# The second expert gets a token list of its own; the table's weight columns are written ahead of the last weight matrix

## The chip, the cores and the metric

The kernel runs on one core of a Trainium2 chip. TensorE (PE) multiplies, VectorE (DVE) and ScalarE (ACT) work elementwise, GpSimd (POOL) works elementwise and issues the gathers and scatters, SyncE (SP) only issues transfers. The metric is the device time of one launch in microseconds (us).

## The reference

The input is q, k, v of 4 batches, 8 heads, 768 steps, 64 per head. Three layers follow one another; the third is the one that the change touches.

```python
# 1: attention with a decaying state; x is its output, 3072 tokens x 512
state = gamma * state + k[t] (outer) v[t];  y[t] = scale * q[t] @ state
# 2: soft mixture, 8 experts x 4 slots
logits = x @ phi;  d = softmax(logits, over tokens)
slot_out[e] = relu((d.T @ x)[e] @ w1[e]) @ w2[e]
x = softmax(logits, over slots) @ slot_out              # rank 32: c @ slot_out
# 3: two of 8 experts for each token
noisy = x @ w_gate + log1p(exp(x @ w_noise)) * noise
top2, weights = the two largest of noisy, softmax of the two
for e in range(8):
    for k in range(2):
        mask = top2[:, k] == e
        out[mask] += weights[mask, k] * (relu(x[mask] @ w1[e]) @ w2[e])
```

## The kernel before, in words

Layers 1 and 2 fill the first 170 us and are not changed. Since x is `c @ slot_out`, the kernel never forms x for layer 3: a table in DRAM (`ctab`) holds for each token its 32 slot weights c and, in 8 more columns, its weight for each expert. G[e] = slot_out @ w1[e] (`g_dot`, with `V1[e]` as the loaded w1[e]) has 32 rows; an expert's hidden layer is the gathered rows of c times G[e].

**Routing** (lines 664 to 741). Matmuls give the noisy logits; DVE finds both experts of each token (`sels`, `tops`); a matmul with constant matrices (`pp`, line 723) numbers the tokens of each expert. ACT, POOL and DVE make the two weights, and SP writes the 8 weight columns (`wsl`) into the table with two transfers (line 741). SP has issued the loads of V1[0], V1[1], V2[0] and V1[2] (2 MB each, V2 in four pieces; lines 647 to 650) ahead of that write; `V2[e]` is w2[e]. V1[0] and V1[1] lie in the ring of buffers `ringa`, V1[2] in `ringp`, which has two.

**Lists** (`lists`, line 819, and `lists_all`, line 845). An expert's list holds its tokens in blocks of 128. It is made by comparing the place of each token with a table (`oh`, three DVE instructions), by marking the block (`bm`, `bt`), and by 24 small matmuls into `pli`; `ls` are the token numbers. Expert 0 has a list of its own (line 1066). The other seven are made at once by `lists_all`, in two passes of 24 matmuls, on DVE and POOL; an entry says too whether the token's other expert comes earlier (`base`, from `order`, `by_turn`, `lead`, `late`), since an expert either writes an output row or adds to it. `order` sorts experts 3 to 7 by their counts.

**Blocks.** Expert 0 has six blocks of 128 and one of 64 in three groups (g = 0, 1, 2). `fetch(e, g)` gathers the table's rows by indirect transfers on POOL's queue, one for each block (line 923). `turn(e, g)` casts and splits them into two parts (ACT, then `st` on DVE), transposes them on PE (`ptc`) and copies them back (ACT, `cts`). `hidden(e, g)` multiplies by G[e] (`phc`), and ACT (relu) and DVE (`hhl`, the remainder) take each result out. `main(e, g)` is, for each block, 8 steps (kf) of three matmuls of 512 columns: `hhl` by the high part `wh` of V2 (lines 1030, 1032) and by its low part `wl` (line 1031). `split_hi` (ACT) and `split_lo` (DVE) make `wh` and `wl` from V2 in four pieces. Then ACT scales by the weight (`yo`), and POOL scatters the rows to the output (line 1005).

**Order.** A planner arranges each engine's instructions by its own costs; `after(ins)` makes what stands in the block follow `ins` where both run on one engine, without a wait. Each engine then runs in that order. `HOOK[e, b, kf]` calls a function when the matmuls of expert e, block b, step kf are written down. Before the change `lists_all` starts ahead of expert 0's blocks (line 1096) and goes on at (0,1,4) and (0,2,2); the second of these also calls the fetches of expert 1. `turn(0, 2)` hangs at (0,0,4). `fill` writes matmuls on a constant whose result nobody reads: F4 = 16 of them after `g_dot(0)` (line 687), FA = 6 and FT = 3 around `g_dot(2)` (lines 1079 to 1082). `gs0`, the spread form of G[0], is made from `gw` (lines 1069 to 1074) after expert 0's list; for the other experts 16 small transfers on SP do it (`gs<-gr`, line 765).

Of the kernel before, what the change touches and what calls it, by code (L numbers as in the profile page):

```python
# [21 lines left out]
P = 128  # L22
# [5 lines left out]
E = 8  # L28
# [13 lines left out]
F1, F2, F3, F4 = 2, 0, 0, 16  # L42
FA, FT = 6, 3
# [4 lines left out]
TZ = 0, 4  # L48
# [59 lines left out]
def kernel(ctx: ExitStack, tc: tile.TileContext, q, k, v, phi, w1, w2,  # L108
# [458 lines left out]
    with rctx, bctx:  # L567
# [88 lines left out]
        first = parts.tile([P, 2, NCH], F16, name="first")  # L656
# [27 lines left out]
        nc.scalar.copy(gr[:, 0], gd)  # L684
        nc.gpsimd.tensor_tensor(gr[:, 1], gd, gr[:, 0], op=OP.subtract)
        with after(mm):
            fill(psB, "pw", F4, 1)
        lo = small.tile([P, NCH, E], F32, name="lo")
# [21 lines left out]
        nc.gpsimd.tensor_tensor(dif, sels[0], sels[1], op=OP.subtract)  # L710
# [13 lines left out]
        ppe = pp[:, :NCH * E].rearrange("p (c e) -> p e c", e=E)[:, 0]  # L724
# [7 lines left out]
        nc.scalar.activation(w[:, 0], w[:, 0], AF.Exp)  # L732
# [6 lines left out]
        nc.gpsimd.tensor_tensor(wsl, wsl, wse, op=OP.add)  # L739
        for r in range(2):  # L740
            nc.sync.dma_start(row_view(r)[:, :, NS:], wsl[64 * r:64 * r + 64])
# [12 lines left out]
    def g_split(pg):  # L754
        gr = cc.tile([P, 2, QF], F32R, name="gr1", bufs=1)
# [11 lines left out]
    def g_one(e):  # L767
        pg = psC.tile([P, QF], F32, name="pg", tag="phc", bufs=4)
        mm = g_dot(e, pg)
        yield mm  # L770
        g_copy(e, g_split(pg))
        yield mm
# [6 lines left out]
    SRC = {}  # L779

    def order():
# [18 lines left out]
        by_turn = cc.tile([P, NCH, E], F16, name="by_turn", bufs=1)  # L800
        nc.gpsimd.tensor_tensor(by_turn, dif, turns[:, None, :].to_broadcast([P, NCH, E]), op=OP.mult)
        lead = cc.tile([P, NCH], F32, name="lead", bufs=1)
        nc.vector.reduce_sum(lead, by_turn, axis=AX.X)
        for i, side in enumerate((OP.is_gt, OP.is_lt)):
            late = cc.tile([P, NCH], F32, name="late")
            nc.gpsimd.tensor_scalar(late, lead, 0.0, float(LATER), op0=side, op1=OP.mult)
            nc.gpsimd.tensor_tensor(base[i], late, col16("base"), op=OP.add)
# [11 lines left out]
    def lists(e, pool, ps, nb, src=None, ahead=()):  # L819
        rv, bv = src or (rr.rearrange("p (e c) -> p e c", e=E)[:, e],  # L820
                         blk.rearrange("p (c e) -> p c e", e=E)[:, :, e])
        bm = pool.tile([P, NCH, nb], F16, name="bm", bufs=1)
# [3 lines left out]
        nc.vector.tensor_tensor(bt[:, :, 0, :], bm, col16("base")[:, :, None].to_broadcast([P, NCH, nb]), op=OP.mult)  # L826
        scaled = nc.scalar.activation(bt[:, :, 1, :], bm, AF.Copy, scale=tokens)
        oh = pool.tile([P, NCH // 8, P, 8], F16, name="oh", bufs=1)
        for c in range(NCH // 8):
            nc.vector.tensor_tensor(oh[:, c], tab, rv[:, None, 8 * c:8 * c + 8].to_broadcast([P, P, 8]),  # L830
                                    op=OP.is_equal)
        hold = [next(a) for a in ahead]
        pl = ps.tile([P, 2, nb], F32, name="pli", tag="pt")
        for c in range(NCH):
            with after(*hold):
                mm = nc.tensor.matmul(pl.rearrange("p a b -> p (a b)"), oh[:, c // 8, :, c % 8],
                                      bt[:, c].rearrange("p a b -> p (a b)"), start=(c == 0), stop=(c == NCH - 1))
        lt = pool.tile([P, nb], F32, name="lt", bufs=1)
        nc.vector.tensor_scalar_add(lt, pl[:, 0, :], float(N))
        ls = pool.tile([P, nb], I32, name="ls", bufs=1)  # L840
        last = nc.vector.tensor_tensor(ls, lt, pl[:, 1, :], op=OP.add)
        LS[e] = FIRST[e] = ls
        return mm, last, scaled

    def lists_all():
        rv = rr.rearrange("p (e c) -> p c e", e=E)
        bv = blk.rearrange("p (c e) -> p c e", e=E)
        pl = psC.tile([P, 2, E, LB], F32, name="pli", tag="pt")
        bm = cc.tile([P, NCH, E, LB], F16, name="bma", bufs=1)
        nc.vector.tensor_tensor(bm, bv[:, :, :, None].to_broadcast([P, NCH, E, LB]),  # L850
                                col16("iotab")[:, None, None, :LB].to_broadcast([P, NCH, E, LB]), op=OP.is_equal)
        for i in range(2):
            rk = cc.tile([P, NCH, E], F16, name="rk")
            nc.vector.tensor_tensor(rk, sels[i], rv, op=OP.mult)
            rs = cc.tile([P, NCH], F32, name="rs")
            nc.vector.reduce_sum(rs, rk, axis=AX.X)
            rh = cc.tile([P, NCH], F16, name="rh")
            nc.vector.tensor_copy(rh, rs)
# [4 lines left out]
            bt = cc.tile([P, NCH, 2, E, LB], F16, name="bta", bufs=1)  # L863
            sb = cc.tile([P, 2, NCH, E], F16, name="sb")
            for a, part in enumerate((base[i], col16("tok"))):
                nc.gpsimd.tensor_tensor(sb[:, a], sels[i], part[:, :, None].to_broadcast([P, NCH, E]),
                                        op=OP.mult)
                eng = nc.gpsimd if a else nc.vector
                eng.tensor_tensor(bt[:, :, a], bm, sb[:, a, :, :, None].to_broadcast([P, NCH, E, LB]), op=OP.mult)
# [5 lines left out]
        lt = cc.tile([P, E, LB], F32, name="lta", bufs=1)  # L875
        nc.vector.tensor_scalar_add(lt, pl[:, 0], float(N))
        ls = cc.tile([P, E, LB], I32, name="lsa", bufs=1)
        nc.vector.tensor_tensor(ls[:, :ES], lt[:, :ES], pl[:, 1, :ES], op=OP.add)
# [33 lines left out]
    def listed(gen):  # L912
        next(gen)
        for g in range(G):
            fetch(1, g)
# [292 lines left out]
```

## Time and profile before

| | |
|---|---|
| runs | 548.7, 548.73, 551.08 us; median 548.73 |
| profiled execution | 550.95 us; span of its instructions 549.1 us |
| PE busy | 511.1 us (93%), mean granted clock 0.961 |
| DVE, ACT, POOL busy | 249.4, 227.6, 247.7 us (45%, 41%, 45%) |
| HBM | 87.89 MB read, 23.43 MB written |

All times below are of the profiled execution, counted from its first instruction. The granted clock is a share of TensorE's full rate. In a timeline row the bracket is the idle time of the engine before the instruction, and what ended it.

### The profile page before, as it was taken

How to read it: one execution, taken by the hardware profiler on the slowest of the kernel's cores; microseconds unless marked ns; L12 is line 12 of the kernel's file. 1: busy time of each engine (PE TensorE's matmuls, PEld its weight loads, DVE VectorE, ACT ScalarE, POOL GpSimd, SP SyncE). 2: the span in 40 equal slices, each digit the busy share in tenths (PEclk: the TensorE clock that was granted, in tenths of full speed). 3: DMA queues.
4: the chain of work that ended last, by engine and by line, in shares of the span. 5: the costliest groups of instructions: out<-in, count | busy, mean ns of one | idle time of the engine just before them, and what ended most of it. 6: DMA issues, size and time to landing. Idle time of an engine off the chain costs nothing.

```text
span 549.1 us, 11659 instructions
## 1 busy us (share of the span) xinstructions
PE 511.1 (93%) x4633; PEld 395.0 (72%) x4633; DVE 249.4 (45%) x505; ACT 227.6 (41%) x496; POOL 247.7 (45%) x245
## 2 busy tenths in 40 slices
PE   5999999998999877969999999999999999999991
PEld 3888788885534456748787788788787877878880
DVE  2878797954032857814415334333324234154100
ACT  3675656542022542325336346345436255164210
POOL 2744644411011357371556667656538544253231
PEclk8899999999997888889999999999999999999996
DMA  9999999998999813153346356456467563563332
GB/s 247 291 305 312 268 308 324 365 407 286 398 408 386 266 43 103 62 191 99 87 153 196 85 177 186 110 157 193 113 167 223 100 178 53 115 155 45 46 44 35
DMA packets 79905, 105.51 MB, mean 192 GB/s; under 512 B 13420, under 2 KB 54892, under 8 KB 79330
## 3 DMA queue, kind: packets, MB, share of 16 engines
q1 hardware_dynamic: 67312, 90.13, 50.8%
q0 software_dynamic: 11856, 14.36, 13.7%
q8 instruction: 38, 0.62, 0.5%
q10 hardware_dynamic: 674, 0.20, 0.3%
q14 instruction: 25, 0.20, 0.1%
HBM read 87.89 MB, written 23.43 MB: 203 GB/s over the span
## 4 chain that ended last, share of the span: by engine, by line
PE 60%; issue 15%; POOL 8%; DMA 7%; DVE 4%; SPq 2%; ACT 2%; POOLq 0%; DVEq 0%; ACTq 0%
PE pyc L1030 9%; PE pyc L1031 9%; PE pyc L1032 9%; POOL out_dram L1005 6%; PE pa L298 4%; PE py L328 4%; PE phc L985 3%; PE ph L559 3%; DMA w<-in_moe_w_dram 3%; PE pS L343 2%; PE pt L286 2%; PE pt L351 2%; PE pt L274 2%; PE py L319 2%; PE po L626 1%
## 5 line engine op out<-in xcount | busy, mean ns | idle before, releaser
L1030 PE MATMUL pyc<-wh,hhl 128*128 128x512 f32 x384 | 153.2, 399 | 1.1 <-ACT yo L1039 1.1
L1031 PE MATMUL pyc<-wl,hhl 128*128 128x512 f32 x384 | 150.9, 393 | 0.0
L1032 PE MATMUL pyc<-wh,hhl 128*128 128x512 f32 x384 | 150.6, 393 | 0.0
L990 DVE SCALAR_TENSOR_TENSOR hhl<-phc,hhl 128x512 fp32r<-128x512 f32 (+1 forms) x112 | 63.3, 606 | 58.2 <-ACT hhl L988 57.8
L1005 POOL DMA_INDIRECT out_dram<-yo,of_second x45 | 70.3, 1562 | 36.0 <-ACT yo L1039 19.9
L1030 PEld LDWEIGHTS pyc<-wh,hhl 128*128 128x128 f32 x384 | 73.1, 190 | 16.0 <-ACT yo L1039 1.9
L1032 PEld LDWEIGHTS pyc<-wh,hhl 128*128 128x128 f32 x384 | 72.7, 189 | 15.1
L1031 PEld LDWEIGHTS pyc<-wl,hhl 128*128 128x128 f32 x384 | 72.9, 190 | 13.7
L966 DVE TENSOR_TENSOR wl<-w,wh 128x1024 fp32r<-128x1024 f32 x32 | 38.9, 1224 | 87.0 <-ACT wh L960 86.1
L1005 POOL DMA_INDIRECT out_dram<-yo,lsa x39 | 41.3, 1060 | 77.8 <-ACT yo L1039 56.3
L988 ACT ACTIVATE hhl<-phc 128x512 fp32r<-128x512 f32 (+1 forms) x112 | 54.6, 549 | 13.3 <-PE phc L985 12.9
L923 POOL DMA_INDIRECT cg<-ctab,of_token x45 | 43.5, 967 | 20.6 <-issue 17.4
L960 ACT CAST wh<-w 128x1024 fp32r<-128x1024 f32 x32 | 33.5, 1052 | 44.5 <-DMA w<-in_moe_w_dram 37.3
L1039 ACT ACTIVATE yo<-pyc,wt 128x512 f32<-128x512 f32 x30 | 20.6, 688 | 69.9 <-PE pyc L1032 66.1
L302 DVE TENSOR_TENSOR am<-pa,cta 128x512 f32<-128x512 f32 x48 | 33.0, 691 | 17.0 <-PE py L328 8.4
L261 POOL TENSOR_TENSOR comp<-raws,cta 64x512 f32<-64x512 f32 x24 | 24.9, 1039 | 30.7 <-PE py L328 14.7
L985 PE MATMUL phc<-cts,gs 128*128 128x256 f32 (+1 forms) x192 | 34.5, 305 | 4.0 <-ACT cts L954 4.0
L261 POOL TENSOR_TENSOR vl<-raws,cta 64x512 f32<-64x512 f32 x24 | 24.9, 1039 | 28.1 <-PE py L328 20.5
L279 DVE TENSOR_TENSOR qT<-pt,cta 64x512 f32<-64x512 f32 x48 | 33.0, 688 | 8.4 <-DMA cta<-in_const_a_dram 6.0
L985 PEld LDWEIGHTS phc<-cts,gs 128*128 128x128 f32 x192 | 29.7, 200 | 9.6 <-ACT cts L954 4.6
L1039 ACT ACTIVATE yo<-pyc,cg 128x512 f32<-128x512 f32 x18 | 12.4, 689 | 43.1 <-PE pyc L1032 39.2
L298 PE MATMUL pa<-qT,kT 64*64 64x128 f32 x768 | 27.4, 282 | 1.1 <-ACT kT L288 1.1
(228 smaller groups left out, 643.8 us busy)
## 6 DMA issues: line engine op xcount, KB each, us to landing
w<-in_moe_w_dram SPq DMA_DIRECT2D x81, 512.0 KB
w<-in_moe_w_dram SPq DMA_DIRECT2D x6, 2048.0 KB
comp<-in_q_dram SPq DMA_DIRECT2D x12, 512.0 KB
raws<-in_k_dram SPq DMA_DIRECT2D x12, 512.0 KB
raws<-in_v_dram SPq DMA_DIRECT2D x12, 512.0 KB
w2q<-in_moe_w_dram SPq DMA_DIRECT2D x8, 512.0 KB
gs<-gr SPq DMA_DIRECT2D x112, 32.0 KB
raws<-in_moe_w_dram SPq DMA_DIRECT2D x2, 1024.0 KB
```

Of the source, the lines that this page charges most:

```text
L261: pool_ins[0] = nc.gpsimd.tensor_tensor(VL[j][rs], RAW[u][1][gs, :, r, :], gv[gs, r, t, :, None].to_broadcast([64, H, D]), op=OP.mult)
L298: mm = nc.tensor.matmul(pa[a][cs, kb, :], KT[j][r, kb, cs], QT[t][r, kb, g, :], start=True, stop=True, skip_group_check=True)
L923: nc.gpsimd.indirect_dma_start(out=cg[:rows(b), i, :], out_offset=None, in_=ctab, in_offset=index(e, b, rows(b)))
L960: ins = nc.scalar.copy(wh, V2[e][:, 1024 * i:1024 * i + 1024])
L966: nc.vector.tensor_tensor(wl, V2[e][:, 1024 * i:1024 * i + 1024], WH[e][i], op=OP.subtract)
L985: nc.tensor.matmul(ph[:, w * i:w * i + w], GS[e][:, kf + i], CT[e, g][:, :w], start=True, stop=True)
L988: relu.append(nc.scalar.activation(h[:, :, :w], pv, AF.Relu))
L990: last = nc.vector.scalar_tensor_tensor(h[:, :, w + t0:w + t0 + 2 * P], pv[:, :, :2 * P], 0.0, h[:, :, :2 * P], op0=OP.max, op1=OP.subtract)
L1005: ins = nc.gpsimd.indirect_dma_start(out=out, out_offset=index(e, b, n, of), in_=y, in_offset=None, bounds_check=N - 1, oob_is_err=False, ...
L1030: nc.tensor.matmul(py, hhl[:, kf, ts], wh, start=(kf == 0), stop=False)
L1031: nc.tensor.matmul(py, hhl[:, kf, ts], wl, start=False, stop=False)
L1032: nc.tensor.matmul(py, hhl[:, kf, tl], wh, start=False, stop=(kf == KF - 1))
```

## The change

The whole of it concerns the stretch from the end of layer 2 to the first blocks of expert 1.

- V2[0] is loaded after the two writes of the weight columns; V1[0] goes to `ringa`, V1[1] and V1[2] to `ringp`.
- `gw` and `gs0` of expert 0 come right after `g_dot(0)` and five fills, ahead of the routing's numbering and of the copies of the counts (`pos`, `cnt`). F4 is 5 instead of 16, five fills (F6) follow `pp`, FA and FT are gone. The ACT instruction of the weights follows the split of G[0].
- POOL makes the weights first; `dif` and two small instructions for `second` (the base of expert 1's list) come after them.
- Expert 1 gets a list by `lists`, with `second` as its base; `apart` takes its two parts. `lists_all` makes the other six (`EJ`), wholly on DVE and ACT (no POOL), in seven steps (`LISTING`), each behind the latest `hidden` on its engine.
- `turn(0, 0)` follows the third cast and the second remainder of V2[0]; the other pieces follow later. The fetches of expert 1 hang at (0,1,3), (0,2,2), (0,3,6), those of expert 2 at (1,2,1); `turn(0, 2)` at (0,1,2).

```diff
-F1, F2, F3, F4 = 2, 0, 0, 16
-FA, FT = 6, 3
+F1, F2, F3, F4, F5, F6 = 2, 0, 0, 5, 0, 5
+LISTING = (0, 1, 6), (0, 2, 3), (0, 2, 5), (0, 4, 3), (0, 4, 6), (0, 5, 3), (1, 0, 4)
-TZ = 0, 4
+TZ = 1, 2
-        for e in range(2):
-            load_w(V1, v1, e, nc.sync, ringa)
-        load_w(V2, v2, 0, nc.sync, ringb)
-        load_w(V1, v1, 2, nc.sync, ringp)
+        for e, ring in enumerate((ringa, ringp, ringp)):
+            load_w(V1, v1, e, nc.sync, ring)
...
             fill(psB, "pw", F4, 1)
+            for g in range(4):
+                gw = psB.tile([P, QF], F32, name="gw", tag="pt")
...
+                nc.scalar.copy(gs0[:, g], gw)
...
-        nc.scalar.activation(w[:, 0], w[:, 0], AF.Exp)
+        with after(split):
+            nc.scalar.activation(w[:, 0], w[:, 0], AF.Exp)
...
         for r in range(2):
-            nc.sync.dma_start(row_view(r)[:, :, NS:], wsl[64 * r:64 * r + 64])
+            written = nc.sync.dma_start(row_view(r)[:, :, NS:], wsl[64 * r:64 * r + 64])
+        with after(written):
+            load_w(V2, v2, 0, nc.sync, ringb)
+        with after(weighed):
+            nc.gpsimd.tensor_tensor(dif, sels[0], sels[1], op=OP.subtract)
+            nc.gpsimd.tensor_scalar(second, selh.rearrange("p (c e) -> p e c", e=E)[:, 0], float(LATER), 0.0,
+                                    op0=OP.mult, op1=OP.add)
+            nc.gpsimd.tensor_tensor(second, second, col16("base"), op=OP.add)
...
+        turns = TURNS[0]
+        nc.vector.tensor_tensor(by_turn, dif, turns[:, None, :].to_broadcast([P, NCH, E]), op=OP.mult)
+        nc.vector.reduce_sum(lead, by_turn, axis=AX.X)
+        for i, side in enumerate((OP.is_gt, OP.is_lt)):
+            nc.vector.tensor_scalar(late, lead, 0.0, float(LATER), op0=side, op1=OP.mult)
+            nc.vector.tensor_tensor(base[i], late, col16("base"), op=OP.add)
+        wide = [P, NCH, EJ, LB]
         for i in range(2):
+            nc.vector.scalar_tensor_tensor(of, sels[1 - i][:, :, 2:], BIG, bv[:, :, 2:], op0=OP.mult, op1=OP.add)
+            nc.vector.tensor_tensor(bm, of[:, :, :, None].to_broadcast(wide), ..., op=OP.is_equal)
+            nc.scalar.activation(bt[:, :, 1], bm, AF.Copy, scale=tokens)
+            yield
+            nc.vector.tensor_tensor(bt[:, :, 0], bm, base[i][:, :, None, None].to_broadcast(wide), op=OP.mult)
             nc.vector.tensor_tensor(rk, sels[i], rv, op=OP.mult)
+                nc.vector.reduce_sum(rh, rk, axis=AX.X)
+            yield
             for c in range(NCH // 8):
                 nc.vector.tensor_tensor(oh[:, c], tab, ..., op=OP.is_equal)
-                nc.gpsimd.tensor_tensor(sb[:, a], sels[i], part[:, :, None].to_broadcast([P, NCH, E]), op=OP.mult)
-                eng = nc.gpsimd if a else nc.vector
-                eng.tensor_tensor(bt[:, :, a], bm, sb[:, a, :, :, None].to_broadcast([P, NCH, E, LB]), op=OP.mult)
             yield
...
+    g1, l0 = g_one(1), lists(0, cc, psC, LB, (first[:, 1, 0], first[:, 0, 0]))
+    next(l0)
+    made = next(l0)
+    with after(*made):
         fetch(0, 0)
+        mm, _ = g1
+        g2 = g_one(2, "pyc", None)
         with after(mm):
+            mm = next(g2)
+        cast = [split_hi(0, i) for i in range(3)]
+        rest = [split_lo(0, i) for i in range(2)]
+        with after(mm):
+            ga = turn(0, 0, [cast[2], rest[1]])
+        with after(*ga):
+            split_lo(0, 2)
...
+        with after(relu[1]):
+            split_hi(0, 3)
+        with after(h0, relu[-1]):
+            split_lo(0, 3)
+            next(g2)
...
         with after(h0, *ga):
+            l1 = lists(1, cc, psC, LB, (first[:, 1, 1], first[:, 0, 1]), second)
+            next(l1)
...
+            HOOK[0, 1, 1] = lambda: [next(l1), apart(1)],
+            HOOK[0, 1, 5] = behind, order, places
+            for at_b in LISTING:
+                HOOK[at_b] = behind, lambda: next(gen)
+            for g, (at_b, kf) in enumerate(((1, 3), (2, 2), (3, 6))):
+                HOOK[0, at_b, kf] = fetch, 1, g
+            HOOK[1, 2, 1] = lambda: [fetch(2, g) for g in range(G)],
```

## Rows read from the trace of the kernel before

**Rows 1.** Windows: busy time by engine, granted clock, DMA share, GB/s.
```profile
core 0: us, PE busy (x) PEld busy (x) DVE busy (x) ACT busy (x) POOL busy (x), PEclk, DMA share, GB/s
199.10:249.70 50.60, 41.79 (x199) 33.73 (x199) 31.94 (x79) 18.19 (x46) 27.42 (x28) 0.84 0.30 100
...
400.00:500.00 100.00, 98.91 (x518) 80.15 (x517) 35.87 (x68) 45.16 (x100) 48.51 (x38) 1.00 0.56 136
```
**Rows 2.** Chain of waits, 160 to 200 us: start, us, what.
```profile
183.78 5.39 DMA ctab<-wsl
...
189.20 2.36 DVE wl L966 x2
...
193.95 2.45 DMA cg<-ctab,ls
...
199.13 0.79 PE pyc L1030
```
**Rows 3.** Windows around the write of the weight columns.
```profile
183.00:189.00 6.00, 4.64 (x65) 3.29 (x66) 4.88 (x11) 4.05 (x8) 1.24 (x3) 0.94 0.99 287
189.00:192.00 3.00, 3.00 (x9) 1.11 (x9) 3.00 (x4) 2.07 (x6) 0.00 (x0) 0.55 0.19 45
```
**Rows 4.** Timeline of POOL: routing's end, first fetches of experts 0 and 1.
```profile
181.39 0.73 POOL L685 TENSOR_TENSOR gr<-gd,gr 128x256 fp32r<-128x256 f32 x1
182.08 0.54 POOL L710 TENSOR_TENSOR dif<-sel,sel 128x192 f16<-128x192 f16 x1
...
192.25 1.40 POOL L923 DMA_INDIRECT cg<-ctab,ls  x1 [7.93 <-DVE wl L966]
193.95 0.99 POOL L923 DMA_INDIRECT cg<-ctab,ls  x1 [0.30 <-issue]
...
232.56 0.99 POOL L923 DMA_INDIRECT cg<-ctab,of_token  x1 [0.30 <-DVE of_second L889]
```
**Rows 5.** Timeline of PE from the list of expert 0 on.
```profile
183.82 1.93 PE L187 MATMUL pg<-w,sotT 128*32 128x256 f32 x32 [0.96 <-ACT cnt L728]
185.69 1.63 PE L836 MATMUL pli<-bt,oh 128*128 128x14 f16 x24
```
**Rows 6.** The same timeline, waits of over 0.7 us after 199.12.
```profile
216.49 0.74 PE L951 MATMUL ptc<-identr,st 128*128 128x128 f32 x3 [3.04 <-DVE st L937]
...
225.38 0.76 PE L872 MATMUL pli<-bta,oh 128*128 128x112 f16 x9 [0.78 <-DVE bta L869]
...
238.72 0.52 PE L951 MATMUL ptc<-identr,st 128*128 128x128 f32 x3 [1.42 <-DVE st L937]
...
243.69 1.43 PE L985 MATMUL phc<-cts,gs 128*128 128x320 f32 x4 [3.56 <-ACT cts L954]
```
**Rows 7.** Windows of three stretches of expert 0's stage.
```profile
198.50:201.90 3.40, 3.40 (x12) 2.62 (x11) 1.89 (x3) 2.21 (x6) 2.25 (x4) 0.50 0.14 31
215.60:222.40 6.80, 5.91 (x36) 5.35 (x37) 4.62 (x11) 2.78 (x6) 4.61 (x3) 0.50 0.72 236
242.90:249.70 6.80, 6.01 (x17) 4.95 (x18) 3.35 (x13) 3.98 (x11) 2.61 (x3) 0.50 0.17 50
```
**Rows 8.** Timeline of DVE: expert 0's list, then expert 0's stage.
```profile
185.03 1.28 DVE L830 TENSOR_TENSOR oh<-tab,first 128x1024 f16<-128x1024 f16 x2
...
205.28 2.67 DVE L854 TENSOR_TENSOR rk<-sel,rr 128x192 f16<-128x192 f16 x1
...
210.09 1.88 DVE L861 TENSOR_TENSOR oh<-tab,rh 128x1024 f16<-128x1024 f16 x3
...
216.36 0.49 DVE L854 TENSOR_TENSOR rk<-sel,rr 128x192 f16<-128x192 f16 x1
...
219.66 4.19 DVE L861 TENSOR_TENSOR oh<-tab,rh 128x1024 f16<-128x1024 f16 x3 [2.19 <-PE pli L872]
```
**Rows 9.** Groups by form: DVE 180 to 196 us, then ACT 160 to 262 us.
```profile
L966 DVE TENSOR_TENSOR wl<-w,wh 128x1024 fp32r<-128x1024 f32 x4 | 4.6, 1216 | 0.0
L823 DVE TENSOR_TENSOR bm<-first,ct 128x168 f16<-128x168 f16 x1 | 0.7, 741 | 0.0
...
L960 ACT CAST wh<-w 128x1024 fp32r<-128x1024 f32 x8 | 8.2, 1056 | 0.9 <-PE pyc L1032 0.9
```

More of the change, by code (lines that the diff above doesn't have):

```diff
@@ L655 @@
         gr = parts.tile([P, 2, QF], F32R, name="gr")
-        first = parts.tile([P, 2, NCH], F16, name="first")
+        first = parts.tile([P, 2, 2, NCH], F16, name="first")
+        second = parts.tile([P, NCH], F16, name="second")
         pos = parts.tile([P, NCH * E], F32, name="pos")
@@ L687 @@
             fill(psB, "pw", F4, 1)
+            for g in range(4):
+                gw = psB.tile([P, QF], F32, name="gw", tag="pt")
+                for i in range(2):
+                    mm = nc.tensor.matmul(gw, pselr[32 * g:32 * g + 32, i, :], gr[32 * g:32 * g + 32, i],
+                                          start=(i == 0), stop=(i == 1))
+                nc.scalar.copy(gs0[:, g], gw)
+        with after(mm):
+            fill(psB, "pw", F5, 1)
         lo = small.tile([P, NCH, E], F32, name="lo")
@@ L754, in g_split @@
     def g_split(pg):
-        gr = cc.tile([P, 2, QF], F32R, name="gr1", bufs=1)
+        gr = cc.tile([P, 2, QF], F32R, name="gr1", bufs=2)
         nc.scalar.copy(gr[:, 0], pg)
@@ L799, in order @@
         nc.vector.tensor_scalar_add(turns[:, ES:], rank, float(ES))
[L800 to L807, printed above, removed]
+        TURNS.append(turns)
         nc.vector.memset(ends[:, :ES], float(TL))
@@ L995, in hidden @@
         HH[e, g] = hhl
-        return last, relu
+        return last, relu, mm
     ROWS = [[] for _ in range(E + 1)]
@@ L1063, in load_paced @@
         store[n] = t
-    g1 = g_one(1)
-    with after(*lists(0, cc, psC, LB, (first[:, 1], first[:, 0]), [g1])):
+    g1, l0 = g_one(1), lists(0, cc, psC, LB, (first[:, 1, 0], first[:, 0, 0]))
+    next(l0)
+    made = next(l0)
+    with after(*made):
         fetch(0, 0)
-        next(g1)
-        for g in range(4):
-            gw = psC.tile([P, QF], F32, name="gw", tag="phc", bufs=4)
-            for i in range(2):
-                mm = nc.tensor.matmul(gw, pselr[32 * g:32 * g + 32, i, :], gr[32 * g:32 * g + 32, i],
-                                      start=(i == 0), stop=(i == 1))
-            nc.scalar.copy(gs0[:, g], gw)
-        for i in range(4):
-            split_hi(0, i)
-            split_lo(0, i)
-        with after(mm):
-            fill(psC, "pyc", FA)
-            list(g_one(2))
-            ga = turn(0, 0)
-            fill(psC, "pyc", FT)
+        mm, _ = g1
+        g2 = g_one(2, "pyc", None)
+        with after(mm):
+            mm = next(g2)
+        cast = [split_hi(0, i) for i in range(3)]
+        rest = [split_lo(0, i) for i in range(2)]
+        with after(mm):
+            ga = turn(0, 0, [cast[2], rest[1]])
+        with after(*ga):
+            split_lo(0, 2)
         with after(*ga):
@@ L1101 @@
         if e + 1 < E:
-            pre[0] += [(fetch, e + 1, g) for g in range(G)] if e else []
+            pre[0] += [(fetch, e + 1, g) for g in range(G)] if e > 1 else []
             for g, at_b in enumerate(TURN):
@@ L1114 @@
             if g + 1 < G:
-                last, relu = hidden(e, g + 1)
+                last, relu, _ = hidden(e, g + 1)
                 LAST[:] = last, relu[-1]
@@ L1151 @@
                     nc.vector.tensor_copy(ge[:NS, DM * h:DM * h + DM], pg[:NS])
-                lists(e, ov_p, ov_s, NB)
+                list(lists(e, ov_p, ov_s, NB))
                 lse = LS[e]
```

114 lines of the change are left out of this document (60 added, 54 removed).

## The prediction

> **What bounds the kernel now.** I read the page's slices first: PE is busy nine tenths or more almost everywhere, with dips only around 170 to 200 us, around 215 and around 240. Then windows: from 400 to 500 us PE is busy 98.91 of 100 us at granted clock 1.00, while in the stage of expert 0's blocks (199.1 to 249.7) it is busy 41.79 of 50.6 at a mean clock of 0.84 [rows 1]. So after 250 us PE sets the pace, and any us by which PE gets there sooner should come off the end; what has to be read is why PE gets there so late.
>
> The chain of waits through the start shows three links: the write of the weight columns, 5.39 us from issue to landing, then the first gathers, 2.45 us from the second's issue to landing, then the first block matmul at 199.13 [rows 2]. The chain and POOL's row call the idle time before the first gather a wait for the `wl` remainder [rows 2, 4], but that name is the last to come by the profile. The gather reads the table, and the table's weight columns come from SP's queue, where 2 MB of V1[2] were issued ahead of them. The DMA engines are 0.99 busy from 183 to 189 and 0.19 from 189 to 192; 287 GB/s for 6 us is 1.7 MB that was still to be moved when the write was issued [rows 3]. That backlog, less than one 2 MB matrix, is the 5.39 us.
>
> In expert 0's stage the timeline of PE shows four waits above 0.7 us: 3.04, 0.78, 1.42 and 3.56, together 8.80 [rows 6], which is the stage's 50.6 less 41.79 [rows 1]. Two of them name `st` on DVE, one `bta`, one `cts` on ACT. After the first and the last the granted clock is 0.50, that is the 1.2 GHz level [rows 7]: PE is busy 5.91 and 6.01 us there with work that takes half as long at 2.4 GHz, so 2.95 + 3.00 = 5.95 us go. Waits and what follows them cost 14.75 us.
>
> **The change part by part.**
>
> *Order of the loads.* V2[0], 2.1 MB, goes behind the weight columns; the 1.7 MB of backlog is then gone when they are issued. POOL makes them earlier too: G[0]'s remainder (0.73) and `dif` (0.54) leave the stretch before the last add, 1.2 us [rows 4], so the issue moves from 183.78 to about 182.6. For a write on an idle queue there is no row. Bounds: 2.45, the landing of a gather, and 5.39, the write with the backlog [rows 2]; I take 3.5, nearer the first, for two transfers one behind the other: they land at 186.1 instead of about 189.2 to 192. V1[1] and V1[2] now need buffers that layer 2's experts 3 and 4 hold; the queue has other matrices to move until those are free, so I put that at nothing; if the queue ran dry, it would cost up to the same 3 to 5 us, which is a rival below.
>
> *Expert 0's list.* Its 24 matmuls stand on PE behind g_dot(1), which ends at 185.75, and take 1.63 [rows 5]. Now g_dot(1) follows them. They need the comparisons on DVE, which end at 186.3 [rows 8], so they end near 186.9 instead of 187.3, and the list is complete at about 187.4. That is now later than the table, so it releases the first gather. From the first gather to the first block matmul the chain took 199.13 - 192.25 = 6.9 us [rows 2, 4]. From 187.6 that gives 194.5. The bounds of the gain are 0 and 4.9.
>
> *V2[0] is late on purpose.* Its four pieces follow the table at 1.3 us each (2.1 MB at the 400 GB/s of a full queue, four pieces), so the third is there at about 190.1; its cast takes 1.06 [rows 9] and ends at about 191.2. `turn(0, 0)` stands behind this cast on ACT and behind the second remainder (1.22 [rows 9]) on DVE. The gathered rows are due at 187.6 + 4.15 = 191.8. The two meet within 0.6 us; I charge 0.2. Queued behind on ACT are the transposes' copies and the first relu. Piece four is cast behind the second relu (1.06), and its remainder after the last `hhl`; steps 6 and 7 of the first block need them, 12 to 18 matmuls later, so I charge nothing. First block matmul: 194.7, that is **-4.4 us**.
>
> *PE's small work ahead.* G[0]'s spread form (8 matmuls, 4 copies) moves into the wait for the routing, where 16 fills ran; 5 + 5 fills replace 25. PE is idle for either, so no term, but the granted clock may be lower there; the two g_dots (1.93 each at the full rate [rows 5]) then take up to twice that and would end at 194 instead of 191, up to 2 us late. I keep that for the range.
>
> *The list of its own.* Expert 1's 24 matmuls are new on PE: **+1.6** (1.63 in the row for expert 0 [rows 5]; bounds half of it and 2.5). The joint list keeps 48 matmuls of 84 columns instead of 112, which I put at nothing.
>
> *The late steps.* Before, expert 1's gathers waited for the whole joint list at 232.56 [rows 4]. With its own list at the start of block 1 they go out some 15 us before they are needed; the 3.56 wait and the half rate behind it lose their cause. POOL leaves the lists. There it fought with DVE: `rk` took 2.67 once and 0.49 once, the three comparisons 4.19 once and 1.88 once [rows 8], 4.5 us of DVE time in front of the `st` and `bta` that PE waited for. The pieces now stand behind the latest hidden layer on DVE. So all 14.75 us lose the cause that the rows show. But DVE gets full: 31.94 less 4.5 is 27.4; added are expert 1's list (0.74 for `bm` [rows 9], about as much for the rest of the marks and sums, 1.88 for comparisons [rows 8]), two remainders that come after the first block matmul (2 x 1.22), and some 1.2 of POOL's small steps: 34.5 us. PE has 41.79 - 5.95 - 1.4 (the half rate at the start, which stays [rows 7]) + 1.6 = 36.0. Two engines this close, in fixed orders, will wait for each other somewhere. I put back 5.0 us, between the cheapest wait of before (0.8) and the dearest with its stretch at half rate (3.56 + 3.0 = 6.6), nearer the latter because DVE is nearly full: **-9.75**.
>
> *Sum.* -4.4 + 1.6 - 9.75 = -12.55, so the profiled execution goes from 550.95 to 538.4. That execution is 2.2 above the median of the runs, 548.73; the forecast for the median is **536.2 us**. With 0.8 to 6.6 put back and a start 4.9 to 2.5 earlier, this case's own range is 531.5 to 539.7. What follows PE's last matmul is not touched.
>
> **Rivals.**
>
> *DVE becomes the bound of the stage.* 34.5 against 36.0 us leaves no room, and every wait may return in another place. For it: DVE works in its fixed order. Against it: the hidden layers' outputs stand ahead of the list pieces. Only the start and the new matmuls count then: -2.8, **545.9 us**. Chance 15%.
>
> *The first gathers meet the remainders.* The first gather of before ran 1.40 instead of 0.99 while the last `wl` was on DVE [rows 2, 4, 9]. In the new order two remainders run between 188.7 and 191.2, where both gathers of group 0 are issued. If each of them holds a gather up for its 1.22 us, the start is 2.4 us later: **538.6 us**. Against it: the gather of before was issued during such a remainder and lost 0.4, not 1.2. Chance 15%. The Trainium skill, SBUF — State Buffer, section "SBUF: two separate sides", says that DVE with two SBUF inputs and a GpSimd instruction that reads SBUF lock each other out for the whole instruction; by that rule this case holds in full, and the slow `rk` of [rows 8] agrees with it.
>
> *The table is not earlier.* V1[1] and V1[2] wait for their buffers, the backlog comes later and the columns stand behind it as now, or V2[0]'s casts take the gathers' place. The start's 4.4 are lost: **540.6 us**. Against it: the queue is backed up far beyond the time when both buffers come free. Chance 10%.
>
> *Slower: the stage falls to half rate.* Fifteen fills are gone before it, and DVE is nearly full in it. If PE, fed in short bursts, keeps the 1.2 GHz level that follows each longer wait [rows 7], each us of the stage's 36 of work costs one more. It turns into a loss once 12.55 + 5.0 us of work, half of the stage, run at that level; with two thirds of it (24 us) the time is 548.73 - 17.55 + 24 = **555 us**. Against it: between the waits the clock came back each time. Chance 6%.
>
> **How the numbers follow.** Forecast 54%, DVE 15, gathers 15, table 10, half rate 6. The range reaches from 531 (nearly all waits gone) to 545.5 (the DVE rival left out, with the slower one above it). A measurement of this kernel tells about 0.5%, 2.7 us, from no change. Faster by more than that: forecast, gathers and table, and about half of the DVE rival, 0.86; the other half, 0.07, is the same; the half rate and a rest are slower, 0.07.
>
> **What would show it.** The weight columns issued near 182.6 and the first gather near 187.6, not 192; the first block matmul at 194 to 195.5; expert 1's gathers issued within two blocks of it; no wait of PE above 1.5 us before expert 1's first hidden layer, and not more than one stretch at clock 0.50 after the first; DVE busy over 85% of expert 0's stage; `rk` and the comparisons at 0.5 and 0.65 each. It is wrong if the first gather waits for V2[0] or for a remainder, if PE's waits name `hhl` or the casts of V2[0], or if the clock stays at 0.50 through the blocks.

## The result, and the profile after

The changed kernel ran in 534.85 to 537.58 us, median 535.64, against a median of 549.9 for the kernel before on the same chip: ratio 0.974, 95% interval 0.970 to 0.979. The forecast was 536.2. Run again beside the experiments, on their chips, it gave 0.983 (0.977 to 0.990) and 0.973 (0.969 to 0.976). The profiled execution took 534.85 us, its span 533.1, at a mean granted clock of 0.973. The sum came out as forecast; the two large terms behind it were both mis-sized, in opposite directions, and nearly cancelled.

Windows of the changed kernel: expert 0's stage over the 117 block matmuls that the window of before holds, and to the end of expert 0's blocks; five stretches around the write of the weight columns; and 100 us later on (columns as in [rows 1]).

```profile
core 0: us, PE busy (x) PEld busy (x) DVE busy (x) ACT busy (x) POOL busy (x), PEclk, DMA share, GB/s
198.40:232.30 33.90, 33.90 (x174) 27.66 (x174) 28.89 (x91) 19.68 (x52) 12.59 (x14) 0.97 0.40 130
198.40:244.30 45.90, 45.90 (x247) 37.60 (x247) 35.57 (x100) 25.58 (x61) 14.51 (x16) 0.98 0.41 137
183.00:189.00 6.00, 5.67 (x61) 3.61 (x65) 3.31 (x10) 0.76 (x3) 1.50 (x4) 0.69 0.70 174
184.00:186.00 2.00, 2.00 (x7) 0.66 (x5) 1.92 (x6) 0.76 (x3) 0.00 (x0) 0.50 0.74 55
186.50:192.30 5.80, 4.62 (x82) 2.92 (x80) 2.53 (x6) 2.84 (x4) 3.47 (x3) 0.98 1.00 363
189.00:192.00 3.00, 2.12 (x40) 1.04 (x32) 1.61 (x3) 2.54 (x4) 2.40 (x3) 1.00 1.05 396
192.00:195.00 3.00, 0.00 (x0) 0.00 (x0) 1.18 (x2) 0.80 (x2) 2.50 (x4) 0.76 0.33 86
400.00:500.00 100.00, 100.00 (x524) 81.68 (x523) 36.00 (x65) 44.11 (x93) 45.62 (x36) 1.00 0.52 118
```

The first row answers to [rows 1]: for the same 117 block matmuls PE was busy 41.79 of 50.6 us and is now busy 33.90 of 33.90, at 0.97 instead of 0.84; the joint list's matmuls mostly come later now. All four waits of [rows 6] and both half-rate stretches inside the stage [rows 7] are gone, though DVE is busy 28.89 of these 33.9 us (85%; 77% in the longer window of the second row). The third to seventh row answer to [rows 3]: from 184 to 186 the engines move the weight columns (busy 0.74 at 55 GB/s), from 186.5 to 192.3 they carry V2[0] (2.1 MB at 363 GB/s); before, they were 0.19 busy from 189 to 192. The last row shows a further 1.1 us in 100 (98.91 before), which the prediction did not have; in two later executions of the changed kernel PE is busy 99.77 and 99.63 us there.

The chain of waits from the routing's end to the first block matmul (start, us, what; it answers to [rows 2]):

```profile
182.44 0.39 PE pt L724 x2
...
184.01 2.13 PE pw L146 x5
186.14 1.40 PE pli L845 x24
...
187.77 0.18 DVE ls L850
...
188.22 0.14 POOL cg L951
188.36 1.26 issue
189.62 5.23 DMA cg<-ctab,ls
...
196.52 2.08 PE phc L1014 x8
198.60 0.43 PE pyc L1059
```

The gather is no longer released by the table but by the list (`ls`), as forecast, and starts 4 us earlier than before, 3.3 of them behind the routing's end. Its rows, however, take 5.23 us from issue to landing instead of 2.45. That it is both gathers is in the summary of the table's readers on POOL from 187 to 190.5 us:

```profile
L951 POOL DMA_INDIRECT cg<-ctab,ls x2: 966/1032/1097, 188.2 to 189.6; - x2
...
DMA to landing us min/median/max: 5.2/5.2/5.2
```

Timeline of POOL and, in the fence after it, of DVE in the changed kernel (answering to [rows 4] and [rows 8]):

```profile
188.22 1.10 POOL L951 DMA_INDIRECT cg<-ctab,ls  x1 [4.35 <-DVE ls L850]
189.62 0.97 POOL L951 DMA_INDIRECT cg<-ctab,ls  x1 [0.30 <-issue]
190.89 1.97 POOL L951 DMA_INDIRECT cg<-ctab,ls  x1 [0.30 <-issue]
...
209.45 0.98 POOL L951 DMA_INDIRECT cg<-ctab,of_token  x1 [0.90 <-DVE more L802]
```

```profile
190.81 2.36 DVE L994 TENSOR_TENSOR wl<-w,wh 128x1024 fp32r<-128x1024 f32 x2 [0.52 <-ACT wh L988]
...
220.12 0.50 DVE L893 TENSOR_TENSOR rk<-sel,rr 128x192 f16<-128x192 f16 x1
220.54 0.35 DVE L965 TENSOR_TENSOR st<-cg,cts 128x192 fp32r<-128x192 f32 x1
...
222.20 1.89 DVE L900 TENSOR_TENSOR oh<-tab,rh 128x1024 f16<-128x1024 f16 x3
```

Expert 1's gathers go out at 209.45 instead of 232.56, and `rk` takes 0.50, three `oh` 1.89, each time.

### The profile page after: what moved, and what is told of

Same layout as the page of the kernel before. It is cut to its first block, busy times and chain, and to the rows that moved or that the text cites. A ratio compares the mean times of both kernels' runs of the same rounds, so it can differ in the third digit from the quotient of the medians.

```text
span 533.1 us, 11678 instructions
## 1 busy us (share of the span) xinstructions
PE 503.0 (94%) x4642; PEld 391.2 (73%) x4642; DVE 247.0 (46%) x520; ACT 229.2 (43%) x499; POOL 238.8 (45%) x236
## 4 chain that ended last, share of the span: by engine, by line
PE 68%; issue 14%; POOL 6%; DMA 4%; SPq 3%; ACT 2%; DVE 1%; POOLq 0%; ACTq 0%
PE pyc L1059 11%; PE pyc L1060 10%; PE pyc L1061 10%; POOL out_dram L1034 5%; PE pa L298 4%; PE py L328 4%; PE phc L1014 3%; PE ph L559 3%; PE pt L286 2%; PE pS L343 2%; PE po L626 2%; SPq L781 2%; PE pt L351 2%; PE py L319 2%; PE pt L274 2%
## 5 line engine op out<-in xcount | busy, mean ns | idle before, releaser
L1034 POOL DMA_INDIRECT out_dram<-yo,lsa x32 | 33.7, 1052 | 64.2 <-ACT yo L1068 49.2
L1014 PE MATMUL phc<-cts,gs 128*128 128x256 f32 (+1 forms) x192 | 32.6, 296 | 0.5 <-ACT cts L982 0.5
L1014 PEld LDWEIGHTS phc<-cts,gs 128*128 128x128 f32 x192 | 28.5, 195 | 5.8 <-issue 2.1
L1034 POOL DMA_INDIRECT out_dram<-yo,ls x14 | 15.2, 1088 | 35.5 <-ACT w L1078 15.8
```

The costliest lines, as they stand in the source:

```text
L1014: mm = nc.tensor.matmul(ph[:, w * i:w * i + w], GS[e][:, kf + i], CT[e, g][:, :w], start=True, stop=True)
L1034: ins = nc.gpsimd.indirect_dma_start(out=out, out_offset=index(e, b, n, of), in_=y, in_offset=None, bounds_check=N - 1, oob_is_err=False, ...
```

## The experiments

The time at which the routing ends moves by up to 6.6 us from one execution to another: `selh`, the last step of the choice, starts between 178.8 and 185.4 us, and between 178.8 and 184.1 in three executions of the changed kernel alone. So the table counts from there: from `selh` to the first gather, from the first gather to the first block matmul, and from the first to the fifteenth block that ACT takes out of PSUM, which covers experts 0 and 1. These are of the profiled executions; the ratio is to the kernel before on the same chip, over the timed runs.

| kernel | ratio | routing to gather | gather to block matmul | 15 blocks |
|---|---|---|---|---|
| before | 1 | 11.2 | 6.9 | 101.4 |
| changed | 0.974 | 7.9 | 10.2 | 88.5 |
| changed, group 2 | 0.983 | 8.3 | 10.3 | 88.9 |
| changed, group 3 | 0.973 | 7.7 | 9.4 | 88.8 |
| V2[0] first (group 1) | 0.986 | 12.5 | 7.2 | 90.0 |
| half of V2[0] (1) | 0.976 | 7.7 | 12.7 | 88.9 |
| fills before the blocks (1) | 0.985 | 8.1 | 13.3 | 95.4 |
| G[0]'s copies last (1) | 0.988 | 9.7 | 14.4 | 93.5 |
| marks on POOL (2) | 0.980 | 8.2 | 12.8 | 88.7 |
| half of V2[0] behind the gathers (2) | 0.984 | 7.8 | 9.6 | 92.4 |
| the same, numbering first (2) | 0.984 | 8.4 | 9.1 | 91.7 |
| numbering first, piece four late (3) | 0.977 | 8.5 | 8.6 | 89.6 |
| no own list (3) | 0.981 | 8.0 | 9.0 | 93.0 |
| crowded steps (3) | 0.977 | 7.8 | 10.7 | 88.8 |

The intervals are about 0.004 to either side in group 3 and 0.006 in groups 1 and 2, so most of what follows rests on the rows and not on the ratios.

### The start

**The order of the loads alone.**

```diff
-            load_w(V2, v2, 0, nc.sync, ringb)      # behind the weight columns
+        load_w(V2, v2, 0, nc.sync, ringb)          # behind V1[1], ahead of V1[2]
```

> The changed kernel with one part undone: V2[0] is loaded before V1[2] and the weight columns, as before the change. Theory A (behind the columns V2[0] shares the DMA engines with expert 0's first gathers, and the gathers lose there what the earlier table won): the columns land near 191 again, the first gather is issued near 191.5 and its pair lands 2.5 us after the second's issue, near 195.5 against 194.8, so the first block matmul is within 1 us of the changed kernel's 198.6 and the time within 1.5 us of it. Theory B (the new order of the loads is worth the 4.4 us of the forecast, and something else in the start took them): the first block matmul comes 3 to 4 us later and the time is 539 to 540 us.

The first gather came 12.5 us after `selh` instead of 7.9, and then the first block matmul 7.2 us after it instead of 10.2. The chain shows the trade: the columns wait for 2 MB again, and the gather lands on quiet engines.

```profile
183.29 8.39 DMA ctab<-wsl
192.65 0.30 POOL cg L951
194.05 2.21 DMA cg<-ctab,ls
```

So the new order bought 4.6 us at the gather and gave 3.0 back behind it; the 1.6 that are left are neither theory's size, and no more than the changed kernel's own executions differ (17.1 to 18.6 us from routing to block matmul). In this order the gather waits for the load queue, whose date need not move with `selh`: counted from the span's start the first block matmul comes at 199.82, and at 199.12 in the kernel before. In group 2 a wait of PE of 1.57 stood behind an ACT instruction that had itself been held for 2.41 us, with the releaser `remote` (see the next run).

**Half of V2[0]'s bytes** (the other half is set to zero and not loaded).

```diff
+            for i in range(1, KF, 2):
+                nc.sync.dma_start(hv[:, i:i + 1], hs[:, i:i + 1])
```

> The changed kernel with half the bytes of V2[0] loaded behind the weight columns (every other row block; the rest of the tile is zeroed on POOL some 10 us earlier, so this half of expert 0's products is left out). Theory A (the gathers wait for V2[0] on the DMA engines): 1 MB less is 2.6 us less ahead of them, the second gather lands 2.5 to 3.5 us after its issue instead of 5.2, and the first block matmul comes 1 to 2.5 us earlier; it is held next by the remainders. Theory C (the remainders on DVE hold POOL up, or the list alone sets the start): landing and start as in the changed kernel, time within 0.5 us of it.

Inconclusive. The first gather came when it does in the changed kernel, but the start was later, because ACT stood still for 3.26 us between `st` and the transposes' copy, a pause whose releaser the profile calls `remote`, no engine of the core:

```profile
198.05 0.37 ACT L986 CAST cts<-ptc 128x256 fp32r<-128x256 f32 x1 [3.26 <-remote]
```

The same pause (3.30) stands in the run with the marks on POOL. Other ACT instructions have such pauses in the run before (2.41) and in the run with G[0]'s copies last (7.2 in three pieces, and 2.37); none is in the kernel before or in the three executions of the changed kernel, from 160 to 320 us. Their cause stays open.

**Two pieces of V2[0] behind the gathers.**

```diff
...
+        with after(got):                           # got: the second gather
+            for i in range(4, KF, 2):
+                nc.gpsimd.dma_start(tv[:, i:i + 2], sv[:, i:i + 2])
```

> Pieces three and four of V2[0] (1 MB) are issued on POOL's queue right behind the first two gathers; the third cast follows the transposes' copy. Theory A (the first gathers land late, 5.2 instead of 2.45 us after the second's issue, because V2[0] fills the DMA engines just then): landing 2.5 to 3.2 us after issue, first block matmul at 195.5 to 196.8 instead of 198.4, time 1.5 to 3 us under the changed kernel, less what the late third and fourth pieces cost (up to 1 us, as a PE wait on a cast of wh or on wl in the first block). Rival B (the landing is slow because the gathered rows were just written or because the remainders hold POOL): landing stays near 5 us and the start stays within 0.7 us of 198.4.

**The same, and G[0]'s spread form behind the numbering.**

> The edit of the run before, and G[0]'s spread form (8 small matmuls, 4 copies) moved behind the numbering matmuls. Theory A: the numbering no longer waits 1.8 us for the copies of G[0], the list of expert 0 ends near 186.2 instead of 188.0, and the table's weight columns (187.2) become what releases the first gather: first gather at 187.3, first block matmul another 0.8 to 1.0 us earlier than in the run before, 194.7 to 196. Rival B: the first gather is released by the table anyway and the list was not on the path: start and time as in the run before within 0.3 us. Rival C: the copies of G[0] now stand late on ACT and hold the casts of V2[0], as in the run where they were behind g_dot(2): start 1 us or more later.

**Only piece four late, numbering first** (the diff is to the run above), with the casts and `turn(0, 0)` as in the changed kernel.

```diff
-            for i in range(4, KF, 2):
+            for i in range(6, KF, 2):
```

> G[0]'s spread form behind the numbering matmuls, and only piece four of V2[0] on POOL's queue behind the first two gathers; the order of ACT, DVE and PE in expert 0's blocks is the changed kernel's. Theory A (two causes of the late start: the list 1.8 us late behind the copies of G[0], and the gathers landing late beside V2[0]): first gather 1 us earlier, landing about 1.3 us sooner after issue (3.9 instead of 5.2), first block matmul 1.5 to 2.3 us earlier, no new PE wait over 0.8 us, time 1 to 2.3 us under the changed kernel. Rival B (DVE paces expert 0's stage, since its st stood only 0.8 us ahead of the transposes in group 2): the start is earlier, but a wait before the transposes of group 2 and a stretch at 0.50 behind it give it back: time within 0.7 us or 1 to 3 us above. Rival C: the landing stays at 5 us because three pieces are still ahead of the gathers: start 0 to 0.7 us earlier.

The last of these bears on the landing. The summary of its first two gathers (187 to 190.3 us):

```profile
L952 POOL DMA_INDIRECT cg<-ctab,ls x2: 966/1034/1102, 187.8 to 189.3; - x2
...
DMA to landing us min/median/max: 2.5/2.5/2.5
```

With 0.5 MB of V2[0] moved behind them the gathers land in 2.5 us, as before the change; with it ahead they take 5.2 and 5.3 in two executions of the changed kernel. No row gives the landing with two pieces late. The run also moves the two remainders on DVE (`wl`, from 191.79 on), but they don't fit the landings: in five executions with all of V2[0] ahead (the changed kernel in the first and third group, marks on POOL, no own list, crowded steps) the rows land 2.3 to 2.7 us after V2[0]'s bytes end (the rate falls below 200 GB/s), and anything from 0.0 to 2.7 us after the second remainder ends. So the late rows are V2[0]'s doing; this half of theory A holds, and by more than it expected of one piece (3.9). The other half does not: the first gather comes 0.8 us later behind the routing's end than in the changed kernel of the same group, and though the block matmul is 0.8 us nearer to it (8.6 against 9.4), it comes 17.2 us behind the routing's end, against 17.1. The chain of this run names what is late next:

```profile
182.46 1.06 PE gw L728 x3
183.52 2.25 PE pw L146 x5
185.77 1.40 PE pli L846 x24
187.17 3.25 PE pg L187 x32
...
190.44 0.04 ACT gr L773
...
190.71 0.93 ACT wh L990
191.65 1.99 ACT wh L990 x2
193.64 0.15 ACT cts L965
```

g_dot(1), at a mean clock of 0.58 (3.25 us on the chain for 32 matmuls, 1.93 at nearly the full rate [rows 3, 5]), holds its copy on ACT, the three casts of V2[0] queue behind that copy, and the gathered rows' cast behind the casts. The list did not come earlier either: the numbering began sooner, but the 8 matmuls of G[0] now stood, with the five fills (2.25 us at half rate), between it and the list. In the blocks a wait of 0.92 came up, `ptc` behind `st`, where the changed kernel has 1.12 us from the start of `st` to the start of `ptc`. The time is 0.3% above the changed kernel's of the same group, which is no difference.

With two pieces late the start came 17.4 and 17.5 us behind the routing's end, against 18.6 in the changed kernel of that group, but the fifteen blocks took about 3 us more, and the medians (544.0 and 543.0 against 542.3) show no gain. In the blocks ACT stood idle before a `yo` and before the first relu of group 2; in the changed kernel the two stand in the same order without a wait (213.78 and 214.36). The row of `yo` names `phc`, whose matmuls had ended 1.3 us earlier, so what held ACT is not shown. Timeline of ACT in the kernel with both edits:

```profile
215.02 0.69 ACT L1070 ACTIVATE yo<-pyc,cg 128x512 f32<-128x512 f32 x1 [1.76 <-PE phc L1016]
216.40 0.44 ACT L1019 ACTIVATE hhl<-phc 128x320 fp32r<-128x320 f32 x1 [0.69 <-PE pyc L1061]
```

**G[0]'s spread form behind g_dot(2).**

```diff
-            for g in range(4):                     # behind g_dot(0)
-                gw = psB.tile(...)                 # 8 matmuls, 4 copies into gs0
+        with after(mm):                            # mm: g_dot(2)
+            for g in range(4):
+                gw = psC.tile(...)
```

> The changed kernel with G[0]'s spread form (8 matmuls, 4 copies) taken out of the routing and put behind g_dot(2). The matmul that starts the numbering of the tokens then stands behind nothing on PE and comes at 180.7 instead of 182.4, the list is ready 1.7 us sooner and the table (187.2) releases the first gather, 1 us sooner. Theory A (V2[0] on the DMA engines sets the landing): the gathers land within 0.5 us of 194.8 all the same, time within 0.7 us of the changed kernel. Rival (the list's date sets the start): the first block matmul and the end come 1 us sooner.

Neither theory was tested. The list was ready sooner (185.54, 6.3 us behind the end of the routing; 7.6 in the changed kernel), but the first gather left at 188.92, and its row names `gr` on DVE, not the list or the table. The copies of G[0] ended on ACT at 196.86 and the casts began there, so the start was 4 us later than in the changed kernel (14.4 instead of 10.2 behind the gather). But the matmuls that they copy had ended at 190.86; the copies lost 7.2 us in pauses with the releaser `remote`. A wait of 2.37 before the transposes of expert 1's first group, behind another such pause, cost another 5 us in the blocks. So whether G[0]'s copies stand right in the change is not shown.

**Twenty fills between g_dot(2) and the first transposes.**

```diff
+        with after(mm):
+            fill(psC, "pyc", 20)
```

> The changed kernel with 20 matmuls on a constant after g_dot(2), in the 4.5 us in which PE waits for the gathered rows. If the half rate from 193.6 to 200.4 follows that wait, the clock is 1.00 from the transposes on: they and the first hidden layer take 1.5 us less, six block matmuls 1.2 less, and the time falls by 1.5 to 2.5 us, to about 533.5. If the rate in that stretch does not depend on what PE did during the wait, the start and the time stay within 0.5 us.

The clock was 1.00 from 190 us through the first hidden layer, whose 8 matmuls took 1.20 instead of 2.08 us. But the fills themselves delayed it: they stand on the chain from 191.5 to 198.6, with 2.0 us of pauses among them. In the blocks ACT stood still for 5.63 us among the relus of group 2, which put `hhl` and `st` off on DVE; its row names block matmuls, and why it needed them isn't shown. The wait behind it cost more than the fills could bring (ACT, then PE):

```profile
222.92 0.77 ACT L1017 ACTIVATE hhl<-phc 128x320 fp32r<-128x320 f32 x2 [5.63 <-PE pyc L1061]
```

```profile
227.93 0.71 PE L979 MATMUL ptc<-identr,st 128*128 128x128 f32 x3 [3.96 <-DVE st L965]
```

Windows of the same kernel, its blocks from the first matmul on: PE is busy 42.04 of 46 us at 0.93. What the clock alone is worth is not shown.

```profile
200.30:246.30 46.00, 42.04 (x216) 33.50 (x216) 32.90 (x97) 21.41 (x55) 12.58 (x13) 0.93 0.36 110
```

### The blocks

> The changed kernel itself, beside the experiments of this group. Every theory expects what its first trace showed: 2 to 3% under the kernel before, first block matmul near 198.5 us, no PE wait over 0.5 us from there to 244 us, granted clock 1.00 from about 200.5 us on. If waits or stretches at 0.50 come back here, what the other runs show of them is not due to their edits.

> The changed kernel itself, as the measure for the other runs of this group: 2 to 3% under the kernel before, first expert's stage without a PE wait over 0.5 us.

The first came out at 1.7% instead of 2 to 3, the second as expected; in both there is no wait of PE above 0.5 us from the first hidden layer to the end of expert 0's blocks, clock 1.00 from 204.2 and 199.3 us on.

**The marks of the joint list on POOL.**

```diff
-            nc.scalar.activation(bt[:, :, 1], bm, AF.Copy, scale=tokens)
+            nc.gpsimd.tensor_tensor(sb, sels[i][:, :, 2:], ..., op=OP.mult)
+            nc.gpsimd.tensor_tensor(bt[:, :, 1], bm, ..., op=OP.mult)
```

> The token marks of the joint list (bta, two instructions of 128x1008) go from ACT back to POOL; the order on DVE and PE stays as it is. Theory A (what the change recovered in expert 0's stage came from taking POOL off the lists, because DVE's two-input f16 instructions stall while POOL works): rk, oh or the bta of DVE that stand beside a POOL mark take two to five times their 0.5, 0.68 and 1 us, PE waits 1 to 4 us for one of them or for st behind them, some of it followed by a stretch at 0.50, and the time is 2 to 6 us above the changed kernel. Rival B (the waits went because the list comes in small late steps): DVE rows are stretched by some us, but PE still waits under 0.5 us, and the time is within 1 us.

Rival B. POOL's second mark and DVE's first comparison beside it, in this kernel's two timelines:

```profile
237.76 2.87 POOL L892 TENSOR_TENSOR bta<-bma,sb 128x1008 f16<-128x1008 f16 x1 [0.78 <-PE pli L907]
```

```profile
238.77 2.41 DVE L903 TENSOR_TENSOR oh<-tab,rh 128x1024 f16<-128x1024 f16 x1
```

The comparison takes 2.41 instead of 0.68 us. The Trainium skill, SBUF — State Buffer, section "SBUF: two separate sides", says that a DVE instruction with two SBUF inputs and a GpSimd instruction that reads SBUF lock each other out for a whole instruction; the rows agree, since the comparison ends at 241.18, 0.55 us after the mark (240.63). Yet PE does not feel it: the fifteen blocks take 88.7 us against 88.9, and PE is busy without a break. The run puts back two marks, not the small steps (`late`, `base`, the other `sb`) that POOL had too.

```profile
200.10:246.10 46.00, 46.00 (x244) 37.54 (x243) 36.98 (x99) 23.19 (x59) 19.46 (x16) 0.96 0.41 127
```

**The steps of the joint list close together.**

```diff
-LISTING = (0, 1, 6), (0, 2, 3), (0, 2, 5), (0, 4, 3), (0, 4, 6), (0, 5, 3), (1, 0, 4)
+LISTING = (0, 1, 6), (0, 1, 7), (0, 2, 0), (0, 2, 3), (0, 2, 4), (0, 2, 5), (0, 3, 0)
```

> The seven steps of the joint list follow each other between (0,1,6) and (0,3,0) instead of reaching to (1,0,4); each still stands behind the latest hidden layer. Theory A (what keeps PE fed is that DVE's list work is spread): DVE has the third comparison and both marks ahead of st and hhl of group 2, PE waits 1.5 to 4 us there with a stretch at 0.50, time 2 to 6 us above the changed kernel. Rival B (it is the order behind the hidden layers, not the spreading): no wait over 0.8 us and the time within 1 us.

Rival B again, in the blocks: PE busy 46.00 of 46.00 us, fifteen blocks in 88.8.

```profile
203.90:249.90 46.00, 46.00 (x265) 37.80 (x264) 35.37 (x106) 24.51 (x60) 18.95 (x17) 0.99 0.40 123
```

Its median is 0.6% above the changed kernel's, more than rival B's 1 us; the profiled execution lost its time ahead of `selh` (185.4 us, the latest of all), not in the blocks. Why the layers ahead were slow there isn't shown, and the other executions have no rows.

**No own list for expert 1.**

```diff
-LISTING = (0, 1, 6), (0, 2, 3), (0, 2, 5), (0, 4, 3), (0, 4, 6), (0, 5, 3), (1, 0, 4)
+LISTING = (0, 0, 4), (0, 0, 6), (0, 1, 0), (0, 1, 4), (0, 1, 5), (0, 1, 6), (0, 2, 2)
-    EJ = E - 2
+    EJ = E - 1
...
-            for g, (at_b, kf) in enumerate(((1, 3), (2, 2), (3, 6))):
+            for g, (at_b, kf) in enumerate(((2, 4), (3, 0), (3, 6))):
```

> Expert 1 loses its own list: the joint list holds seven experts again, on DVE and ACT, in seven steps from block 0 to block 2, and expert 1's gathers hang at (0,2,4), (0,3,0), (0,3,6). 24 small matmuls are gone from PE (1.6 us). Theory A (the own list is what took the waits away): the seven steps stand in the first blocks, st of groups 1 and 2 comes behind them, PE waits 1 to 4 us in two or three places with stretches at 0.50, and the time is 3 to 8 us above the changed kernel. Rival B (it is enough that the steps are small and stand behind the hidden layers): no wait over 0.8 us, and the time is within 1 us of the changed kernel or up to 1.6 us below it.

Theory A in the size, not in the place. No `st` stood behind the list's steps. There is one wait, and a stretch at 0.50 from 239.6 to 243.0 us behind it:

```profile
238.22 0.51 PE L979 MATMUL ptc<-identr,st 128*128 128x128 f32 x3 [3.48 <-DVE st L965]
```

`st` waits for the cast of expert 1's gathered rows, and these gathers leave POOL from 231.05 us on, behind the joint list (complete at 228.7) and a scatter:

```profile
229.76 0.98 POOL L1034 DMA_INDIRECT out_dram<-yo,ls  x1 [6.84 <-ACT w L1078]
231.05 0.99 POOL L951 DMA_INDIRECT cg<-ctab,of_token  x1 [0.30 <-issue]
```

The fifteen blocks take 93.0 us, 4.2 more than in the changed kernel of the same group, though 24 matmuls of 1.6 us are gone from them. So what the own list buys in this order is the early gather of expert 1's rows, some 5 to 6 us.

## Why the prediction was right, and where it was wrong

That 536.2 lies 0.6 us from the median is in part luck: the start gave 4.4 us less than forecast and the waits 4.7 more, and the two errors cancelled.

**The start term, -4.4, was wrong.** From the end of the routing to the first block matmul it is 18.0 us before (one execution) and 17.1, 18.0 and 18.6 in three executions after: nothing, within a us. The step that failed is "From 187.6 that gives 194.5": the 6.9 us from the first gather to the first block matmul were carried over from a trace in which the DMA engines were 0.22 busy beside the gathers (192 to 195 us), into one in which V2[0] runs beside them. The steps before it held: columns issued at 182.79 (182.6 forecast), first gather at 188.22 (187.6; five fills at half rate, 2.13 us, stand right ahead of the list). Then the rows took 2.8 us longer than the copied 2.45, and from the rows to the first block matmul it took 3.5 instead of 2.7 us: the granted clock was 0.50 from 193.6, within PE's wait of 4.46 us, to 200.4. (In the third group's execution of the same kernel, at 0.98 there, it took 2.7.) The prediction's own sign of being wrong, "if the first gather waits for V2[0]", came in substance: not its issue, but its rows wait. The prediction had seen the meeting of V2[0]'s pieces with the rows' cast on ACT and had not seen it on the DMA engines.

**The waits, -9.75, were too small.** The 14.75 us that the rows showed came back nearly whole: the fifteen blocks went from 101.36 to 88.53 us, that is 12.8 less, with 1.6 us of new matmuls in them, so 14.4. The step that failed is "Two engines this close, in fixed orders, will wait for each other somewhere", with 5.0 us put back. DVE was full, if less so than forecast (28.89 of 33.9 us over the same block matmuls, 85%; forecast 34.5 of 36.0), but a busy share doesn't make a wait. What makes one, in the rows here, is what stands ahead of an `st` or an `hhl` in the fixed order (a list piece, a late gather, a pause of ACT), and by how much; in this order the nearest `st` came in time. The size of the price was not far off: five of the edited kernels took 2.8 to 6.8 us more for the fifteen blocks, each with waits of 1.4 to 4 us, three of them with a stretch at 0.50 behind one.

**The cause of the waits, "POOL leaves the lists", is not shown.** POOL did slow DVE, but in the changed order marks on POOL cost PE nothing, and neither did crowding the steps. Early gathers for expert 1 are shown to be worth 5 to 6 us, about the 3.56 wait and its half rate [rows 6, 7]. What removed the 3.04 wait of group 2 (the steps' place behind the hidden layers, the later begin of the list, or POOL) was not taken apart and stays open. POOL had a part in it before: `bta`, which stood on DVE ahead of that `st` (216.09), waited for POOL's `sb`, and no run puts POOL's small steps back.

```profile
213.12 1.85 DVE L869 TENSOR_TENSOR bta<-bma,sb 128x1344 f16<-128x1344 f16 x1 [1.16 <-POOL sb L866]
```

**The rest.** Of the 16.0 us by which the span fell, the routing's end gave 0.7, the start nothing, the first block 0.8 (8.1 instead of 8.9 us to its `yo`, since the half rate ended sooner), the fifteen blocks 12.8 and the later experts 1.6, which no term had; that is 15.9. The median moved by 14.3. Of the signs that were to show it, the issue at 182.79, the gather, expert 1's gathers, `rk`, the comparisons and the absence of waits came as written; the first block matmul (198.4, not 194 to 195.5) did not, and DVE's share, at 85%, stood at the edge of "over 85%".

**The rivals.** DVE as the bound: no, PE has no wait beside a DVE that is 85% busy. The gathers meeting the remainders: the third gather did, 1.97 us beside two of them, but the start needs the first two. The table not earlier: no. Half rate: only at the start. None of them had the mechanism that happened, a gather that shares the engines with the load put behind the table.

No kernel here beats the changed one beyond what the runs can tell. The run with piece four late suggests what would have to come next (five fills fewer ahead of the list, the casts ahead of g_dot(1)'s copy); it wasn't tried.

## What to carry to other kernels

A transfer that is moved behind another one does not vanish: ask what will then run beside it, and do not copy a landing time from a stretch in which the DMA engines were idle. Name the instruction that stands ahead of each operand PE waits for, rather than charge for a busy share; and after each edit read the later rows again, since in five of ten edited kernels a wait some 20 to 40 us behind the edit cost more than the edit brought, in four of them with ACT idle around the relus of group 2.

## What the runs showed of the hardware that was not expected

Two gathers of 128 rows of 40 numbers, 2.5 us from issue to landing on quiet queues, took 5.2 us beside 2 MB of a weight load (396 GB/s), and 2.5 again once its last 0.5 MB was issued behind them. ScalarE stood still for up to 5.1 us with the releaser `remote` in four of ten edited kernels, without a cause that the profile names. And the same instructions ahead of the routing's end took 178.8 to 184.1 us in three executions of one kernel.
